# Talking-heads attention: the first twelve tiles mix the queries instead of the scores

## The chip, the cores and the metric

The kernel runs on one core of one Trainium2 chip. The metric is the device time of one execution in microseconds (us); smaller is better.

## The reference

Attention with mixed heads, then a feed-forward layer, for batch 8, 12 heads, 448 positions and head size 64; the layer goes from 768 to 2048 and back.

```python
scores = 1/sqrt(64) * q @ k.T                          # per batch and head: 448 x 448
scores = einsum('bhij,hg->bgij', scores, w_pre)        # 12 x 12: heads mixed before the softmax
attn   = exp(scores - max) / sum(exp(scores - max))
attn   = einsum('bhij,hg->bgij', attn, w_post)         # heads mixed after it
x      = (attn @ v) with heads side by side            # 3584 x 768
out    = relu(x @ w_in)**2 @ w_out
```

## The kernel before

**Loads.** q, k and v of a batch come in three parts of four heads each, on GpSimd's DMA queue, which turns f32 into bf16 (L76). TensorE transposes two pairs of heads at a time (`turn_unit`, L153), and ScalarE or VectorE copies the result to `qT` and `kT` (L155): 128 partitions are two heads of 64, and there are six such pairs.

**Scores.** A batch's 448 queries are cut into blocks of 128 (the fourth has 64). `score_burst` multiplies a block's queries of some head pairs with all keys (L280, L286 for the fourth block) and copies each head's 128 x 448 scores to a tile `S` (L290 on ScalarE, L292 on VectorE). There are two S buffers, so a block's copies wait until the block two before has been read.

**Tiles.** The mixing works on tiles of 10 queries; a batch has 45 (numbered on through the batches, tile 45 is the first of batch 1). `gather` (L309, L312; SyncE's DMA queue) copies the 10 x 12 rows of 448 scores of a tile from S, where a query is a partition, to a tile `G`, where each of 120 rows is one query of one head. There are twelve G buffers, and the program order has the gather of tile i + 10 behind step i. `mix` then needs one matmul with a 120 x 120 matrix `pre`, which holds `w_pre` for each of the ten queries (L320), an exp with row sums on ScalarE (L323), a reciprocal on VectorE (L325), and on GpSimd the product of that with the matrix `post` (L327). Four steps later (`LAG`), `unmix` multiplies exp with it by four matmuls (L340) and VectorE copies the result (L342). The tiles of the fourth block hold the heads in another order and have their own versions of `pre`, built from further small loads of w_pre (`col_pre`, L99; L107 to L119).

**The rest.** Every 15 tiles `av_unit` multiplies with v (L169). The feed-forward layer of a batch (`ffn1_unit`, L213, L219, L223; `ffn2_unit`, L247) fills TensorE between the tiles of a later batch, by a list with weights in time; batch 0's first half is put in early, from step 21 on (`EARLY`).

**Order.** TensorE's and GpSimd's instructions are issued in the order in which the program writes them; those of the other engines are ordered by a scheduler. A loop over steps emits, for step i: the loads due (`at_load`; GpSimd), `mix` of tile i, units due, filler, `unmix` of tile i - 4, the gather, and, at positions set by `FIRST` and `BURSTS`, half a score burst for the block after the one being gathered. Before the loop, batch 0's q and k are transposed, its first two blocks scored and copied, and ten gathers issued:

```python
        for x in range(2):
            score_burst(0, 1, [3 * x, 3 * x + 1, 3 * x + 2])
        for x in range(AHEAD):
            gather(steps[x])
```

The k and q loads of batch 1 go to the buffers of batch 0's, so they wait for its transposes; w_in (`w1`) and w_out (`w2`) are loaded in eight parts each, at the steps of `W1_AT` and `W2_AT`.

Of the kernel before, what the change touches and what calls it, by code (L numbers as in the profile page):

```python
# [8 lines left out]
BF16 = mybir.dt.bfloat16  # L9
F32 = mybir.dt.float32  # L10
# [33 lines left out]
def kernel(  # L44
# [33 lines left out]

    staged, vs = {}, {}
    staged[0] = (stage_tile("qst", 1), stage_tile("kst", 1))  # L80
    load(staged[0][1], k, 0, 0, 4)
    ident = consts.tile([P, P], BF16, name="ident")
    masks.make_identity(nc, ident[:, :])
    load(staged[0][0], q, 0, 0, 4)
    for x in (4, 8):
        load(staged[0][1], k, 0, x, x + 4)
        load(staged[0][0], q, 0, x, x + 4)

    def split(n0, n):

        rows = [(0, 0, [[0, n0], [H, H]], H * n0)] if n0 else []
        if n > n0:
            rows += [(H * n0 + HALF * (n - n0) * c, HALF * H * c, [[0, n - n0], [H, HALF]], HALF * (n - n0)) for c in range(2)]
        return rows

    def wcol(w, name, eng, n0, n):
        t = consts.tile([P, H], F32, name=name)
        for o, src, ap, rows in split(n0, n):
            eng.dma_start(out=t[o:o + rows, 0:H],  # L99
                          in_=bass.AP(tensor=w.tensor, offset=w[0, 0:1].offset + src, ap=ap + [[1, H]]))  # L100
        return t

    def stripes(name, n0, n):
        t = consts.tile([P, IQ], F32, name=name)
        rg = H * n
        if n0:
            nc.vector.tensor_reduce(out=t[0:rg, 0:n0], in_=ident[0:rg, 0:H * n0].rearrange("p (i h) -> p i h", h=H),  # L107
                                    axis=mybir.AxisListType.X, op=ALU.add)
        if n > n0:
            nc.vector.tensor_reduce(out=t[0:rg, n0:n], in_=ident[0:rg, H * n0:rg].rearrange(  # L110
                "p (c i h) -> p i c h", c=2, h=HALF), axis=mybir.AxisListType.XY, op=ALU.add)
        return t

    def pre_matrix(x, eng, n0, n):
        col = wcol(w_pre, f"col_pre{x}", eng, n0, n)
        st = stripes(f"istripe{x}", n0, n)
        rg = H * n
        t = consts.tile([P, IQ, H], BF16, name=f"pre{x}")
        nc.vector.tensor_tensor(out=t[0:rg, 0:n, :], in0=st[0:rg, 0:n].unsqueeze(2).to_broadcast([rg, n, H]),  # L119
                                in1=col[0:rg, :].unsqueeze(1).to_broadcast([rg, n, H]), op=ALU.mult)  # L120
        return t[:, :, :].rearrange("p i g -> p (i g)"), st

    pre, istripe = pre_matrix(0, nc.sync, IQ, IQ)
    col_post = wcol(w_post, "col_post", nc.scalar, IQ, IQ)
# [12 lines left out]
    w2 = [wts.tile([P, FT // 4, DMODEL], BF16, name=f"w2_{x}") for x in range(4)]  # L137

    qTs, kTs, xts, h2ts, ats = {}, {}, {}, {}, {}

    def turn_unit(b, which, u, eng=None):

# [126 lines left out]
    def score_burst(b, blk, pairs):  # L269

        if (b, blk) not in Sb:
            Sb[(b, blk)] = work.tile([P, H, S], BF16, name="S", tag="S", bufs=2)
        sb = Sb[(b, blk)]
        got = []
        for p in pairs:
            for hh in range(2):
                rs = slice(64 * hh, 64 * hh + 64)
                ps = bank("s_ps")
                if blk < 3:
                    nc.tensor.matmul(ps[:, 0:S], lhsT=qTs[b][rs, p, P * blk:P * blk + P], rhs=kTs[b][rs, p, :],  # L280
                                     start=True, stop=True)
                got.append((2 * p + hh, ps))
            for c in range(2 if blk == 3 else 0):
                for hh in range(2):
                    rs = slice(64 * hh, 64 * hh + 64)
                    nc.tensor.matmul(got[2 * p + hh][1][64 * c:64 * c + 64, 0:S], lhsT=qTs[b][rs, 3 * c + p, P * blk:S],  # L286
                                     rhs=kTs[b][rs, 3 * c + p, :], start=True, stop=True)
        for h, ps in got:
            if h % 2 == 0 or (b == 0 and h in (3, 9)):
                nc.scalar.copy(out=sb[:, h, :], in_=ps[:, 0:S])  # L290
            else:
                nc.vector.tensor_copy(out=sb[:, h, :], in_=ps[:, 0:S])  # L292

    def rows_of(t):
        return H * min(IQ, S - IQ * t)

    def gather(s):

        b, t = s
        g = work.tile([P, S], BF16, name="G", tag="G", bufs=AHEAD + 2)  # L300
        x, end = IQ * t, min(IQ * t + IQ, S)
        while x < end:
            blk = x // P
            n = min(end, P * blk + P) - x
            o, y = H * (x - IQ * t), x - P * blk
            sb = Sb[(b, blk)]
            dst = g[o:o + H * n, :]
            if blk < 3:
                nc.sync.dma_start(out=dst, in_=sb[y:y + n, :, :])  # L309
            else:  # L310
                for c in range(2):
                    nc.sync.dma_start(out=g[o + HALF * n * c:o + HALF * n * c + HALF * n, :],  # L312
                                      in_=sb[64 * c + y:64 * c + y + n, 0:HALF, :])
            x += n
        Gs[s] = g

    def mix(s):
        n = rows_of(s[1])
        ps = bank("m_ps")
# [39 lines left out]
        if not filler:  # L359
            owed[0] = min(owed[0], 0.0)  # L360

    blocks = [(b, blk) for b in range(B) for blk in range(4)]
    steps = [(b, t) for b in range(B) for t in range(NT)]
    with tc.manual_schedule(engines={PE, POOL}):
        for x in range(4):
            if x < 3:
                turn_unit(0, 1, x)
                turn_unit(0, 0, x, nc.scalar.copy)
            if x > 0:
                score_burst(0, 0, [2 * x - 2, 2 * x - 1])  # L370
        for x in range(2):
            score_burst(0, 1, [3 * x, 3 * x + 1, 3 * x + 2])
        for x in range(AHEAD):
            gather(steps[x])
        pres = {}
        for t in range(NT):
            n = min(IQ, S - IQ * t)
            key = (max(0, min(n, 3 * P - IQ * t)), n)
            if key not in pres.values():
                pres[t] = key  # L380
        pres = {t: pre if key == (IQ, IQ) else pre_matrix(t, nc.sync, *key)[0] for t, key in pres.items()}
        loads = {}

        def at_load(i, f, *args):
            loads.setdefault(i, []).append(lambda: f(*args))

        for x in range(3):
            load_v(0, x)
# [21 lines left out]
        for i in range(-1, len(steps) + LAG):  # L410
            for f in loads.get(i, []):
                f()
            if i < 0:
                continue
            s0 = steps[i] if i < len(steps) else None
            s1 = steps[i - LAG] if i >= LAG else None
            if s0:
# [15 lines left out]
            if s1:  # L433
# [4 lines left out]
                        at_step(i + 2, u)  # L438
                if t1 == NT - 1:
                    at_step(i + 2 if b1 else FFN2_AT, (0, lambda b1=b1: filler.extend(ffn_units(b1))))  # L440
            if i + AHEAD < len(steps):
                gather(steps[i + AHEAD])
                b2, t2 = steps[i + AHEAD]
                blk2 = max(x for x in range(4) if FIRST[x] <= t2)
                nxt = 4 * b2 + blk2 + 1
                first = BURSTS[blk2]
                if 1 < nxt < len(blocks) and t2 - FIRST[blk2] in first:
                    x = first.index(t2 - FIRST[blk2])
# [37 lines left out]
```

## Time and profile before

| | us |
|---|---|
| median of 3 runs | 623.85 (623.54 to 625.07) |
| profiled execution | 621.52 |
| its span in the profile | 619.6 |
| TensorE busy | 568.9 (92%) |
| VectorE busy | 403.5 (65%) |
| ScalarE busy | 380.9 (61%) |
| GpSimd busy | 333.0 (54%) |
| gathers (L309, L312) | 368 transfers of 105.0 or 52.5 KB and some smaller |

PE is TensorE's matmuls and PEld its weight loads, DVE is VectorE, ACT ScalarE, POOL GpSimd, SP SyncE. Busy times are unions of intervals, and engines run side by side. Rows of digits cut the span in 40 slices of 15.5 us and give tenths of it busy; PEclk is the clock granted to TensorE in tenths of full speed, DMA the mean busy share of 16 DMA engines (in a short stretch it can go over 1, as packets overlap). In the chain of waits each line has the start, the length and what the end of the kernel waited for; "idle ... <-" or "waited" names what came last. A group's line gives the form, the count, then the busy time in us, the mean of one in ns, and the idle time before it.

### The profile page before, as it was taken

To read this page: it belongs to the slowest core of one execution; us is meant where nothing else is said; L and a number is where in the kernel's file an instruction comes from. 1 tells how busy PE (TensorE), PEld (TensorE's weight loads), DVE (VectorE), ACT (ScalarE), POOL (GpSimd) and SP (SyncE) were. 2 spreads that over 40 slices of the span, in tenths; PEclk is the share of its full clock that TensorE was granted. 3 is DMA by queue.
4 is the path that set the end of the run, shared out by engine and by line. 5 is a ranking of instruction groups with operands and counts; after the bars stand their busy time and mean duration, and the time that the engine had idled before them with its cause. 6 is when DMAs were issued, how large, how long until landed. Compare 5 with 4: busy or idle time off the path is not lost.

```text
span 619.6 us, 17165 instructions
## 1 busy us (share of the span) xinstructions
PE 568.9 (92%) x5960; PEld 366.6 (59%) x5960; DVE 403.5 (65%) x998; ACT 380.9 (61%) x1107; POOL 333.0 (54%) x742
## 2 busy tenths in 40 slices
PE   3657697989999999999999999999999999998996
PEld 2225475656656666656666666656665666665553
DVE  2448574498877778777767778777767677665011
ACT  2746586666677656776577557776578557861410
POOL 4434589736277623794287623793286425751640
PEclk9769799899999999999999999999999999999999
DMA  9999789649856965488446965488543655422002
GB/s 123 144 187 193 146 167 211 96 100 164 190 105 105 143 142 119 76 144 164 106 95 108 150 135 110 80 142 161 119 87 63 118 129 104 87 51 73 7 26 77
DMA packets 91104, 73.51 MB, mean 119 GB/s; under 512 B 7048, under 2 KB 87432, under 8 KB 91016
## 3 DMA queue, kind: packets, MB, share of 16 engines
q1 hardware_dynamic: 52102, 49.59, 34.6%
q0 software_dynamic: 38784, 22.81, 28.7%
q8 instruction: 47, 0.77, 0.5%
q14 instruction: 41, 0.34, 0.1%
q10 hardware_dynamic: 130, 0.01, 0.0%
HBM read 45.64 MB, written 11.01 MB: 91 GB/s over the span
## 4 chain that ended last, share of the span: by engine, by line
PE 79%; DMA 10%; ACT 4%; DVE 2%; POOL 2%; issue 1%; SPq 1%; ACTq 0%; DVEq 0%; POOLq 0%
PE o_ps L247 24%; PE h_ps L213 21%; PE at_ps L340 11%; PE m_ps L320 10%; DMA G<-S 9%; PE ot_ps L169 6%; PE s_ps L280 3%; PE tr_ps L153 3%; ACT S L290 2%; ACT e L323 1%; DMA col_pre<-in_w_pre_dram 1%; PE s_ps L286 1%; DVE at L342 1%; POOL h L223 1%; SPq L99 1%
## 5 line engine op out<-in xcount | busy, mean ns | idle before, releaser
L342 DVE CAST at<-at_ps 112x480 bf16<-112x480 f32 x360 | 227.9, 649 | 69.3 <-PE at_ps L340 68.4
L327 POOL TENSOR_SCALAR pn<-post,rc 120x120 bf16<-120x120 bf16 x360 | 130.5, 365 | 219.4 <-DVE rc L325 130.3
L323 ACT ACTIVATE e<-m_ps 120x448 bf16<-120x448 f32 x360 | 195.6, 549 | 77.1 <-PE m_ps L320 77.1
L213 PE MATMUL h_ps<-xt,w 128*128 128x448 bf16 (+2 forms) x960 | 168.4, 316 | 0.9 <-ACT e L323 0.3
L340 PE MATMUL at_ps<-pn,e 120*128 120x120 bf16 (+1 forms) x1440 | 136.3, 218 | 13.3 <-ACT S L290 11.6
L320 PE MATMUL m_ps<-G,pre 120*120 120x448 bf16 x360 | 131.6, 367 | 12.2 <-DMA G<-S 8.3
L340 PEld LDWEIGHTS <-e 120*128 120x128 bf16 (+1 forms) x1440 | 106.0, 99 | 59.9 <-ACT S L290 15.0
L247 PE MATMUL o_ps<-w,h 128*128 128x384 bf16 x768 | 139.3, 327 | 0.0
L223 POOL TENSOR_TENSOR h<-hr 128x384 bf16<-128x384 f32 (+2 forms) x160 | 111.1, 696 | 29.7 <-ACT hr L219 26.3
L213 PEld LDWEIGHTS <-w 128*128 128x128 bf16 x960 | 84.4, 98 | 55.7 <-issue 5.0
L219 ACT ACTIVATE hr<-h_ps 128x448 f32<-128x448 f32 (+2 forms) x160 | 75.7, 475 | 57.0 <-PE h_ps L213 32.4
L290 ACT CAST S<-s_ps 128x448 bf16<-128x448 f32 x175 | 81.5, 552 | 34.5 <-PE s_ps L280 19.2
L247 PEld LDWEIGHTS <-h 128*128 128x128 bf16 x768 | 73.6, 98 | 48.2 <-issue 5.0
L292 DVE CAST S<-s_ps 128x448 bf16<-128x448 f32 x161 | 90.4, 615 | 16.3 <-DMA G<-S 13.2
L325 DVE RECIPROCAL rc<-sm 120x1 f32<-120x1 f32 x360 | 57.0, 159 | 57.0 <-ACT e L323 46.2
L323 ACT ACTIVATION_READ_ACCUMULATOR e<-m_ps 120x1 f32 x360 | 75.1, 209 | 0.0
L320 PEld LDWEIGHTS <-pre 120*120 120x120 bf16 x360 | 48.6, 135 | 33.1 <-DMA G<-S 14.2
L253 DVE COPY osb<-o_ps 128x384 f32<-128x384 f32 x56 | 31.2, 557 | 55.4 <-PE o_ps L247 55.1
L280 PE MATMUL s_ps<-kT,qT 64*128 64x448 bf16 x288 | 42.0, 364 | 5.1 <-ACT hr L219 3.2
L169 PE MATMUL ot_ps<-at,v 112*64 112x150 bf16 x1152 | 42.0, 228 | 4.4 <-DVE at L342 4.3
L175 ACT CAST xt<-ot_ps 128x450 bf16<-128x450 f32 (+1 forms) x48 | 25.5, 533 | 32.9 <-PE ot_ps L169 32.9
L169 PEld LDWEIGHTS <-v 112*64 112x64 bf16 x1152 | 38.4, 109 | 8.1 <-issue 6.7
(30 smaller groups left out, 248.5 us busy)
## 6 DMA issues: line engine op xcount, KB each, us to landing
G<-S SPq DMA_DIRECT2D x288, 105.0 KB
kst<-in_k_dram POOLq DMA_DIRECT2D x24, 224.0 KB, 5.6
qst<-in_q_dram POOLq DMA_DIRECT2D x24, 224.0 KB, 5.5
v<-in_v_dram POOLq DMA_DIRECT2D x24, 224.0 KB, 6.8
G<-S SPq DMA_DIRECT2D x80, 52.5 KB
w<-in_moe_w_in_dram POOLq DMA_DIRECT2D x8, 384.0 KB, 8.6
w<-in_moe_w_out_dram POOLq DMA_DIRECT2D x8, 384.0 KB, 8.0
out_dram<-osb SPq DMA_DIRECT2D x8, 336.0 KB
```

Source lines behind the costliest of these rows:

```text
L169: nc.tensor.matmul(ps[64 * hh:64 * hh + 64, TQ * y:TQ * y + TQ], lhsT=vs[b][0:PR, g, r, :], rhs=at[0:PR, r, g, :], start=(y == 0 and r == ...
L213: nc.tensor.matmul(ps[:, 0:n], lhsT=w1[ft // 4][:, c2, ft % 4 * 128:ft % 4 * 128 + 128], rhs=xts[b][:, c2, n0:n1], start=(c2 == 0), stop=( ...
L219: nc.scalar.activation(out=hr[:, 0:n], in_=ps[:, 0:n], func=ACT.Relu)
L223: nc.gpsimd.tensor_tensor(out=dst[:, x - o:y - o], in0=hr[:, x - n0:y - n0], in1=hr[:, x - n0:y - n0], op=ALU.mult)
L247: nc.tensor.matmul(ps[:, 0:384], lhsT=lhsT, rhs=w2[ft // 4][:, ft % 4, nt * 384:(nt + 1) * 384], start=(ft == 0), stop=(ft == FT - 1))
L290: nc.scalar.copy(out=sb[:, h, :], in_=ps[:, 0:S])
L292: nc.vector.tensor_copy(out=sb[:, h, :], in_=ps[:, 0:S])
L320: nc.tensor.matmul(ps[0:n, 0:S], lhsT=pres[max(x for x in pres if x <= s[1])][0:n, 0:n], rhs=Gs.pop(s)[0:n, :], start=True, stop=True)
L323: nc.scalar.activation(out=e[0:n, 0:S], in_=ps[0:n, 0:S], func=ACT.Exp, scale=SCALE, accum_out=sm[0:n, 0:1])
L327: nc.gpsimd.tensor_scalar(out=pn[0:n, :], in0=post[0:n, :], scalar1=rc[0:n, 0:1], scalar2=1.0, op0=ALU.mult, op1=ALU.mult)
L340: nc.tensor.matmul(ps[:, RG * r:RG * r + RG], lhsT=e[0:n, PR * r:PR * r + P], rhs=pn[0:n, :], start=True, stop=True)
L342: nc.vector.tensor_copy(out=ats[(b, third)][0:PR, :, :, IQ * tl:IQ * tl + IQ], in_=ps[0:PR, 0:R * RG].rearrange("p (r g i) -> p r g i", r= ...
```

## The change

Mixing the heads' scores with w_pre is the same as mixing the queries first: for output head g, the query of each head h is multiplied by w_pre[h, g], and one product over all heads and their 64 dimensions gives the mixed score. Tiles 0 to 11 (120 queries of batch 0) now do that. `mix_queries` writes `qmix`: per pair of heads and query, twelve versions of the query, one for each g, as a product of `qT` with `wrep`, which holds w_pre's row of each partition's head. Nine such instructions replace the scores of these tiles: for each of three `u` (two pairs of heads), queries 0 to 39 and 40 to 79 on VectorE and 80 to 119 on GpSimd. `mix` of these tiles is then six matmuls, one for each pair of heads, that add up in PSUM; they need no S copies and no gather. qmix lies in the buffers of w_out's first three quarters, which are loaded from step 26 on.

For batch 0 the remaining 328 queries make three blocks of 128, starting at queries 120, 240 and 320, where there were four; none of its tiles is split between blocks, and none has the other order of heads. Its first block is scored in three parts: before step 0, in step 0 and in step 1. Gathers start in the program order of step 6, two in each step until they are ten ahead.

At the start, q is loaded before k in each part, q's copies move to VectorE and k's to ScalarE, and v's loads stand ahead of the mixing on GpSimd. One `col_pre` load stays; the versions of `pre` for the other order of heads are made at step 22 by three small matmuls and copies. `wrep` is loaded by two transfers of 384 rows of 48 bytes each.

```diff
-FIRST = [0, 13, 26, 39, NT]
-BURSTS = [[5, 8], [5, 8], [6], [0, 3]]
+FUSED = 12
+FQ = FUSED * IQ
+QB = (0, 40, 80, FQ)
+STARTS = {0: (FQ, 2 * FQ, S - 128)}
+FIRST = {0: (FUSED, 2 * FUSED, 3 * FUSED)}
+BURSTS = {0: ([5, 8], [5, 8], [3, 6])}
+for _b in range(1, B):
+    STARTS[_b], FIRST[_b], BURSTS[_b] = (0, 128, 256, 384), (0, 13, 26, 39), ([5, 8], [5, 8], [6], [0, 3])
+GATHERS_AT = 6
...
+    wrep = consts.tile([P, NPAIR, H], F32, name="wrep")
+    for hh in range(2):
+        nc.sync.dma_start(out=wrep[64 * hh:64 * hh + 64, :, :],
+                          in_=bass.AP(tensor=w_pre.tensor, offset=w_pre[0, 0:1].offset + H * hh,
+                                      ap=[[0, 64], [2 * H, NPAIR], [1, H]]))
...
+    def mix_queries(u, part, eng):
+        a, n = QB[part], QB[part + 1] - QB[part]
+        eng.tensor_tensor(out=qmix[u][:, :, a:a + n, :],
+                          in0=qTs[0][:, 2 * u:2 * u + 2, a:a + n].unsqueeze(3).to_broadcast([P, 2, n, H]),
+                          in1=wrep[:, 2 * u:2 * u + 2, :].unsqueeze(2).to_broadcast([P, 2, n, H]), op=ALU.mult)
...
     def mix(s):
...
-        nc.tensor.matmul(ps[0:n, 0:S], lhsT=pres[max(x for x in pres if x <= s[1])][0:n, 0:n], rhs=Gs.pop(s)[0:n, :], start=True, stop=True)
+        if b == 0 and t < FUSED:
+            for p in range(NPAIR):
+                nc.tensor.matmul(ps[0:n, 0:S], rhs=kTs[b][:, p, :],
+                                 lhsT=qmix[p // 2][:, p % 2, IQ * t:IQ * t + IQ, :].rearrange("p i g -> p (i g)"),
+                                 start=(p == 0), stop=(p == NPAIR - 1))
+        else:
+            m = pres[max(x for x in pres if x <= t)] if b else pre
+            nc.tensor.matmul(ps[0:n, 0:S], lhsT=m[0:n, 0:n], rhs=Gs.pop(s)[0:n, :], start=True, stop=True)
...
-        for x in range(4):
-            if x < 3:
-                turn_unit(0, 1, x)
-                turn_unit(0, 0, x, nc.scalar.copy)
-            if x > 0:
-                score_burst(0, 0, [2 * x - 2, 2 * x - 1])
-        for x in range(2):
-            score_burst(0, 1, [3 * x, 3 * x + 1, 3 * x + 2])
-        for x in range(AHEAD):
-            gather(steps[x])
+        for x in range(3):
+            load_v(0, x)
+        for u in range(NPAIR // 2):
+            turn_unit(0, 0, u)
+            mix_queries(u, 0, nc.vector)
+            mix_queries(u, 1, nc.vector)
+            if u == 1:
+                score_burst(0, 0, [0, 1])
+            if u < 2:
+                mix_queries(u, 2, nc.gpsimd)
+            turn_unit(0, 1, u, nc.scalar.copy)
...
             if i < 0:
+                mix_queries(2, 2, nc.gpsimd)
                 continue
+            if i == NT // 2:
+                for (_, n), (t, order) in orders.items():
+                    half_pre(n, t, order)
...
-            if i + AHEAD < len(steps):
-                gather(steps[i + AHEAD])
...
+            if i < 2:
+                score_burst(0, 0, [2 + 2 * i, 3 + 2 * i])
+            for _ in range(2 if i >= GATHERS_AT else 0):
+                if ahead[0] > min(i + AHEAD, len(steps) - 1):
+                    break
+                b2, t2 = steps[ahead[0]]
+                gather((b2, t2))
+                ahead[0] += 1
```

More of the change, by code (lines that the diff above doesn't have):

```diff
@@ L96, in wcol @@
-    def wcol(w, name, eng, n0, n):
+    def wcol(w, name, eng):
         t = consts.tile([P, H], F32, name=name)
-        for o, src, ap, rows in split(n0, n):
-            eng.dma_start(out=t[o:o + rows, 0:H],
-                          in_=bass.AP(tensor=w.tensor, offset=w[0, 0:1].offset + src, ap=ap + [[1, H]]))
-        return t
-    def stripes(name, n0, n):
-        t = consts.tile([P, IQ], F32, name=name)
-        rg = H * n
[L106 to L123, printed above, removed]
@@ L124 @@
-    col_post = wcol(w_post, "col_post", nc.scalar, IQ, IQ)
+        src = bass.AP(tensor=w.tensor, offset=w[0, 0:1].offset, ap=[[0, IQ], [H, H], [1, H]])
+        eng.dma_start(out=t[0:RG, 0:H], in_=src)
+        return t
+    col_pre = wcol(w_pre, "col_pre", nc.sync)
+    istripe = consts.tile([P, IQ], F32, name="istripe")
+    nc.vector.tensor_reduce(out=istripe[0:RG, :], in_=ident[0:RG, 0:RG].rearrange("p (i h) -> p i h", h=H),
+                            axis=mybir.AxisListType.X, op=ALU.add)
@@ new lines, with half_order @@
+    pre = consts.tile([P, IQ, H], BF16, name="pre")
+    nc.vector.tensor_tensor(out=pre[0:RG, :, :], in0=istripe[0:RG, :].unsqueeze(2).to_broadcast([RG, IQ, H]),
+                            in1=col_pre[0:RG, :].unsqueeze(1).to_broadcast([RG, IQ, H]), op=ALU.mult)
+    pre = pre[:, :, :].rearrange("p i g -> p (i g)")
+    def half_order(x, n0, n):
+        t = consts.tile([P, RG], BF16, name=f"order{x}")
+        o, rg = H * n0, H * n
+        if n0:
+            nc.vector.tensor_copy(out=t[0:rg, 0:o], in_=ident[0:rg, 0:o])
+        nc.vector.tensor_copy(out=t[0:rg, o:rg].rearrange("p (c i h) -> p c i h", c=2, h=HALF),
+                              in_=ident[0:rg, o:rg].rearrange("p (i c h) -> p c i h", c=2, h=HALF))
+        return t
@@ new lines, with half_pre @@
+    orders, pres = {}, {0: pre}
+    for t in range(3 * P // IQ, NT):
+        n0, n = max(0, 3 * P - IQ * t), min(IQ, S - IQ * t)
+        if (n0, n) not in orders:
+            orders[(n0, n)] = (t, half_order(t, n0, n))
+    def half_pre(n, t, order):
+        rg = H * n
+        ps = bank("pre_ps")
+        nc.tensor.matmul(ps[0:rg, 0:rg], lhsT=order[0:rg, 0:rg], rhs=pre[0:rg, 0:rg], start=True, stop=True)
+        pres[t] = consts.tile([P, RG], BF16, name=f"pre{t}")
+        nc.vector.tensor_copy(out=pres[t][0:rg, 0:rg], in_=ps[0:rg, 0:rg])
```

50 lines of the change are left out of this document (21 added, 29 removed).

## The prediction

> **What bounds the kernel now.** I read the page first, then busy time by stages, the chain of waits of the first 75 us, the waits by engine, and single rows for prices. The page:
>
> ```profile
> span 619.6 us, 17165 instructions
> ...
> PE   3657697989999999999999999999999999998996
> ...
> PEclk9769799899999999999999999999999999999999
> DMA  9999789649856965488446965488543655422002
> ```
>
> PE is full from about the tenth slice (15.5 us each) to the end; before that it has holes, and there the DMA row shows 9. The stages, cut at tiles 0, 12, 23, 31 and 55 (the starts of their L320 matmuls in the timeline: 25.44, 43.85, 57.06, 72.27 and 112.31):
>
> ```profile
> core 0: us, PE busy (x) PEld busy (x) DVE busy (x) ACT busy (x) POOL busy (x), PEclk, DMA share, GB/s
> 0.00:25.40 25.40, 10.12 (x120) 5.73 (x120) 8.63 (x27) 10.98 (x20) 9.85 (x19) 0.96 1.02 134
> 25.40:43.90 18.50, 10.52 (x57) 5.13 (x58) 7.62 (x23) 9.10 (x30) 8.53 (x18) 0.59 0.97 173
> 43.90:57.00 13.10, 11.02 (x213) 7.98 (x211) 10.93 (x30) 8.71 (x27) 6.64 (x15) 1.00 1.00 192
> 57.00:72.30 15.30, 8.33 (x93) 6.18 (x90) 8.23 (x20) 8.36 (x28) 6.79 (x16) 0.86 0.89 178
> 72.30:112.30 40.00, 35.41 (x488) 28.93 (x487) 24.25 (x62) 29.55 (x102) 34.24 (x83) 0.97 0.96 169
> 112.30:600.00 487.70, 479.07 (x4915) 304.12 (x4913) 340.46 (x832) 314.18 (x902) 266.99 (x594) 1.00 0.58 109
> ```
>
> From 112.3 on PE is busy 98% of the time: whatever the start gains or loses is carried to the end. In the first four rows (72.3 us) PE is idle 32.3 us and DMA is at 0.89 to 1.02. The chain says on what, and the waits say through whom:
>
> ```profile
> 17.18 2.21 ACT S L290 x6
> 19.38 6.01 DMA G<-S
> ...
> 32.31 7.65 DMA G<-S
> ...
> 40.65 11.28 DMA G<-S
> ...
> 64.65 5.75 DMA G<-S
> ```
>
> ```profile
> ACT S L290 <- DMA G<-S: 15.2, 3, 7.9
> ```
>
> The gathers hurt twice. Tile 0 can start only when all S copies of block 0 and a first gather (6.01) are through. And S has two buffers: the S copies of a new block wait, in ACT's and DVE's order, until the gathers out of the block two before have landed; exp and unmix copies queue behind them. That is 15.2 us on ACT in three waits (32 to 40, near 57, 65 to 70.5).
>
> **The change part by part.** Five rows give the prices; the second number after the bar is the mean in ns:
>
> ```profile
> L119 DVE TENSOR_TENSOR pre<-istripe,col_pre 120x120 bf16<-120x120 f32 x3 | 0.8, 283 | 7.8 <-DMA col_pre<-in_w_pre_dram 7.8
> ...
> L119 DVE TENSOR_TENSOR pre<-istripe,col_pre 96x96 bf16<-96x96 f32 x1 | 0.3, 255 | 0.3 <-DVE istripe L110 0.3
> ```
>
> ```profile
> L223 POOL TENSOR_TENSOR h<-hr 128x384 bf16<-128x384 f32 x112 | 92.4, 825 | 22.4 <-ACT hr L219 19.1
> ...
> L223 POOL TENSOR_TENSOR tails<-hr 128x64 bf16<-128x64 f32 x128 | 37.0, 289 | 0.0
> ```
>
> ```profile
> 201.82 1.30 PE L213 MATMUL h_ps<-xt,w 128*128 128x448 bf16 x6
> ```
>
> *Mixing the queries.* Nine tensor_tensors of 960 elements, six on DVE, three on POOL. DVE's slope is (283-255)/24 = 1.17 ns an element, so 283 + 840 x 1.17 = 1.26 us each; POOL's is (825-289)/320 = 1.68, so 289 + 896 x 1.68 = 1.79 us each.
>
> *Their weights, wrep.* Two SP transfers, 768 rows of 48 B, take the place of seven col_pre transfers (336 such rows). The first DVE mix waits for both. No row shows this transfer. Lower bound: the first col_pre (120 rows, issued 0.75) was used at 4.67, 3.9 us later; the second wrep would be issued at about 2.6 and with three times the rows land at about 8. Upper bound: from 8.0 to 13.5 us, with the q/k/v loads filling the engines, that queue moved 292 packets, 252 of them such rows, 46 a us; 768 rows from 4.5 us on then land at 21. I take 13 us: the nearest row is the col_pre issued at 4.88, which landed at 12.68, 7.8 us under the same loads. The Trainium skill ("DMA: Bandwidth & Descriptors", section "Why a DMA increments its semaphore by 16 and not by 1") says that a transfer runs on as many engines, up to 16, as divide both sides' slowest dimension: 16 for wrep's 64 partitions against 10 or fewer for col_pre's rows. By that the per-row pace is too pessimistic; no run here shows it yet.
>
> *First tile.* After wrep, DVE does two mixes, a qT copy (0.61), two mixes, a copy, one mix, before PE can end tile 0: 5 x 1.26 + 2 x 0.61 = 7.5 us. Nothing is queued behind it that is due sooner; kT copies now run on ACT. On POOL the b=1 k and q loads stand behind two of its mixes: they are issued near 19 us instead of 15.8, and are first needed at step 14 (tile 14, near 44 us). Whether DVE and POOL mixes run side by side no row shows: between 0 (side by side) and 2 x 1.79 = 3.6 us (POOL first each time) I put one POOL mix, 1.8 us, on the path. The Trainium skill ("SBUF — State Buffer", section "SBUF: two separate sides") speaks against the change here: a DVE instruction with two SBUF inputs and a GpSimd instruction that reads SBUF lock each other out of one port pair for the whole instruction; by it the term is 3.6 and not 1.8. So: 13 + 7.5 + 1.8 + 0.7 for the last cold matmuls = 23.0 for tile 0, against 25.44.
>
> *Tiles 0 to 11.* Six matmuls each. Warm price: the six of L213 at 201.82 have the same 448 columns, and PE's next instruction starts at 202.96, so 0.19 us a matmul, 1.14 a tile; an unmix (202.96 to 203.17) adds 0.21. The granted clock was 0.59 in the second stage above, with PE half idle; here PE is dense, so I count tile 1 and the eight score matmuls beside it at half clock (6 x 0.38, and twice the 0.93 of the four at 13.67: 4.2 us), and ten tiles at full clock: 11.4 + 8 unmixes 1.7 + 12 score matmuls 1.5 (six at 74.71 took 0.74) = 14.6. Tile 12 starts at 23.0 + 4.2 + 14.6 = 41.8, against 43.85: 2 us ahead. The 60 extra matmuls (11.4 us) take the place of PE's idle time; without that cover the change loses them.
>
> *Tiles 12 to 28.* Their gathers can be issued as soon as the first block is copied, near 28.5 us (at 0.86 us each, by the gathers' issue rows), 13 us before they are used. The three waits for a gather at tiles 17, 18 and 20 (0.69 + 0.70 + 0.65) go; a little work comes in (two more S copies on DVE, three small matmuls and copies for half_pre). Before, 18.96 us; I take 18.3, DVE being busy 10.9 of 13.1 us there already. Tile 29 at 60.1 against 62.81.
>
> *The wait at tile 29 to 31.* Before, block (1,0) goes into the buffer of tiles 26 to 38, whose last gather is issued at 64.65 and lands at 70.41; tile 29 to tile 31 takes 9.46 us, with ACT idle 5.34. After, batch 0 has three blocks, the buffer is that of tiles 24 to 35, three gathers earlier, and none of batch 0's gathers is split in two. The gather of tile 35 needs the G buffer of tile 23 (there are twelve), is issued at about 55 and lands, with the same 6 to 8 us, at 61 to 63. I leave 1 us of wait: 4.5 instead of 9.46. Sum at tile 31: 2.7 + 5.0 = 7.7 us ahead.
>
> *A second way to that sum.* The stage is full of DMA: twelve gathers of 105 KB fewer are 1.26 MB, at 171 GB/s (the mean of the first 72 us from 3 us on) 7.4 us.
>
> *Behind tile 31* PE's instructions stand in the same order as before. DMA is at 0.96 and POOL busy 34.24 of 40 us up to tile 55, so loads that now crowd closer may give 1.2 us back. Net 6.5 us: the profiled execution goes from 621.52 to 615.0, and the median of the runs, 2.3 us above that execution, from 623.85 to 617.3.
>
> **The rivals.** *Slower: wrep lands late.* At 21 us tile 0 is through at 32, tile 12 at 50.8 (7 us late), the b=1 loads and all W1 loads are issued 8 us later, since POOL takes them in order behind its mixes, and the wait at tile 31 only gives back 5. That is about 3 us slower, 626.8; it decides from wrep at 18 us on. For it: 46 rows a us beside the loads. Against: those transfers were still being issued until 8.01.
>
> *No change.* Lead given back up to tile 55, because the 17 weight, k, q and v loads of that stage set its time: about 623.5. For: DMA 0.96. Against: PE and POOL hold 35.41 and 34.24 of the 40 us by themselves.
>
> *More.* wrep by 9 us and mixes side by side: tile 0 at 17.2, tile 12 at 36, gathers started near 23 and the wait at tile 31 gone: 11 to 12 us faster, 612.
>
> *Little.* The gather wait at tile 29 stays at 5 us since the gathers start 9 us later than now: 3 us faster, 621.
>
> **How the numbers follow.** Forecast 4 to 9 us faster 0.55, more 0.13, little 0.10, no change 0.10, slower 0.12. 0.3% is 1.9 us, about what a measurement of this kernel can tell from no change: faster 0.78, same 0.10, slower 0.12. The range 612.0 to 624.5 leaves out the slower case and the far end of "more".
>
> **What would show it.** wrep's end as the DVE mix's start (13); first fused matmul's tile done near 23; tile 12 near 42; no ACT wait over 2 us on a gather before 75 us; tile 31 near 64.6; from there the same distance to the end. The forecast is wrong if the first DVE mix starts after 18, if the fused matmuls cost 0.38 us throughout, or if tile 55 has lost the lead of tile 31.

## The result, and the profile after

The changed kernel took 617.16 us (median of 4 runs, 614.54 to 619.12) against 623.69 (4 runs, 621.81 to 625.07): a ratio of 0.9895, interval 0.9848 to 0.9941. Four further sets of runs, each with its own runs of before, stand behind the experiments; in one of them the changed kernel was measured again. The profiled execution took 617.85 us (before: 621.52).

The page after, same rows as before:

```profile
span 616.1 us, 17210 instructions
...
PE   3797988898999999999999999999999999998996
...
PEclk9797998999999999999999999999999999999999
DMA  8997999559647955587547955597544755422002
```

PE's holes are fewer, but not gone: the 7 in the fourth slice (46 to 62 us) is where the lead is spent. The stages, cut at the first fused matmul (16.2) and at tiles 12, 23, 31 and 55 by the start of their matmuls:

```profile
core 0: us, PE busy (x) PEld busy (x) DVE busy (x) ACT busy (x) POOL busy (x), PEclk, DMA share, GB/s
0.00:16.20 16.20, 5.87 (x100) 4.32 (x100) 7.46 (x18) 4.72 (x7) 10.67 (x17) 1.00 0.84 104
16.20:40.80 24.60, 20.85 (x131) 12.17 (x126) 17.27 (x31) 12.90 (x36) 16.19 (x24) 0.86 1.07 158
40.80:59.50 18.70, 14.27 (x218) 10.23 (x216) 12.57 (x35) 10.44 (x33) 6.63 (x16) 0.82 0.84 166
59.50:67.70 8.20, 7.38 (x88) 5.62 (x88) 7.01 (x19) 7.41 (x26) 5.90 (x15) 1.00 0.82 137
67.70:108.30 40.60, 35.97 (x489) 29.72 (x487) 24.68 (x64) 29.60 (x104) 35.52 (x87) 0.96 1.05 189
```

Tiles 12 to 22 (third row) take 18.7 us where they took 13.1, with PE busy 14.27 and its clock down to 0.82; tiles 23 to 30 (fourth row) take 8.2 instead of 15.3. The chain of waits says why (start, length, what was waited for):

```profile
2.56 8.24 DMA wrep<-in_w_pre_dram
10.92 3.84 DVE w L163 x2
14.76 0.55 DVE qT L181
15.33 3.84 DVE w L163 x2
...
42.93 7.99 DMA G<-S
50.95 0.54 ACT S L317
51.53 0.53 PE s_ps L307
52.06 0.56 PE m_ps L355
52.61 3.14 PE ot_ps L195 x47
```

The waits from 15 to 73 us, by engine, have one entry for S on ACT, and PE's next score matmul waits behind it:

```profile
ACT S L317 <- DMA G<-S: 4.3, 1, 4.3
...
PE s_ps L307 <- ACT S L317: 3.7, 1, 3.7
```

Before it was 15.2 us in three waits; now it is one, of 4.3 us, at a place where the prediction had none: ahead of tile 20. The S copies of batch 0's last block go into the buffer that tiles 12 to 23 are gathered from. The last of those gathers, tile 23's, was issued at 38.36, and the copies could start at 50.95, 12.6 us later. The chain names a later gather there (issued at 42.93); the semaphore on which ACT waits last is that of tile 23's gather. Its updates are in the trace: behind a first one at 39.55, nine came from 46.20 to 48.52 and the last at 50.85, which ended the wait. After the stall PE comes back at half clock: the 47 matmuls of `ot_ps` take 3.14 us, and the granted clock is 0.50 from 52.6 to 55.7.

Start of the first matmul of four tiles, in us, in every profile of this study (the kernels are explained below). The medians are from different sets of runs, so they are compared by their ratios; w1_late's ratio leaves out one slow run, of 621.75 us.

| kernel | tile 12 | tile 20 | tile 31 | tile 55 | median | ratio to before |
|---|---|---|---|---|---|---|
| before | 43.85 | 51.97 | 72.27 | 112.31 | 623.69 | 1 |
| after | 40.77 | 51.99 | 67.71 | 108.33 | 617.16 | 0.9895 (0.9848 to 0.9941) |
| after, again | 39.84 | 51.02 | 66.40 | 105.73 | 615.18 | 0.9896 (0.9856 to 0.9935) |
| own_before | 40.37 | 51.64 | 67.08 | 111.84 | 618.65 | 0.9954 (0.9933 to 0.9975) |
| own_after | 40.21 | 47.35 | 61.24 | 102.70 | 613.15 | 0.986 (0.9831 to 0.9889) |
| w1_late | 40.01 | 47.60 | 63.23 | 103.27 | 616.27 | 0.9909 (0.9873 to 0.9946) |
| mix_first | 37.85 | 49.58 | 64.98 | 104.33 | 615.72 | 0.99 (0.9869 to 0.9931) |
| wrep_one | 39.97 | 50.26 | 65.95 | 106.55 | 616.17 | 0.9921 (0.9892 to 0.9949) |
| wrep_pe | 38.04 | 49.07 | 64.83 | 105.43 | 615.81 | 0.9886 (0.9851 to 0.992) |
| dup_thin | 41.01 | 56.98 | 72.16 | 111.64 | 623.31 | 0.9996 (0.9975 to 1.0017) |
| dup12 | 40.66 | 64.32 | 80.50 | 121.52 | 631.51 | 1.015 (1.012 to 1.0179) |
| own_mix | 36.07 | 43.89 | 57.47 | 101.11 | 609.9 | 0.9805 (0.9776 to 0.9834) |
| best | 33.76 | 40.96 | 54.77 | 99.80 | 608.1 | 0.9766 (0.9735 to 0.9796) |
| best_w1 | 33.46 | 41.28 | 54.79 | 100.26 | 610.89 | 0.9819 (0.9788 to 0.9849) |

Two profiles of the same kernel (after, after again) differ by 0.9 us at tile 12 and 2.6 at tile 55, so smaller differences between rows say nothing. Behind tile 55 all kernels have the same program order, yet the 14 profiles take 507.2 to 510.8 us from there to the end. Most of that lies between tiles 55 and 90, where the clock granted to TensorE differs even between two executions of one kernel, here after and after again:

```profile
108.33:153.40 45.07, 39.83 (x484) 26.12 (x482) 36.92 (x95) 30.51 (x95) 22.71 (x57) 1.00 0.75 127
```

```profile
105.73:153.50 47.77, 43.21 (x484) 27.35 (x482) 36.86 (x95) 30.76 (x96) 23.65 (x60) 0.93 0.73 122
```

So "whatever the start gains or loses is carried to the end" holds only within about 3 us for a single execution. Why the clock is lower in one of them is open.

### The profile page after: what moved, and what is told of

It is laid out like the page before. It is cut to its first block, busy times and chain, and to the rows that moved or that the text cites. A ratio compares the mean times of both kernels' runs of the same rounds, so it can differ in the third digit from the quotient of the medians.

```text
span 616.1 us, 17210 instructions
## 1 busy us (share of the span) xinstructions
PE 577.5 (94%) x6011; PEld 375.7 (61%) x6011; DVE 412.7 (67%) x1002; ACT 378.5 (61%) x1103; POOL 340.9 (55%) x745
## 4 chain that ended last, share of the span: by engine, by line
PE 81%; DMA 8%; DVE 4%; ACT 3%; POOL 1%; issue 1%; SPq 0%; ACTq 0%; DVEq 0%
PE o_ps L273 23%; PE h_ps L239 21%; PE at_ps L375 11%; PE m_ps L355 10%; DMA G<-S 7%; PE ot_ps L195 7%; PE s_ps L307 3%; PE tr_ps L179 3%; PE m_ps L350 2%; ACT e L358 2%; DVE w L163 1%; DMA wrep<-in_w_pre_dram 1%; PE s_ps L313 1%; DVE at L377 1%; ACT S L317 1%
## 5 line engine op out<-in xcount | busy, mean ns | idle before, releaser
L375 PE MATMUL at_ps<-pn,e 120*128 120x120 bf16 (+1 forms) x1440 | 134.9, 216 | 0.5 <-ACT hr L245 0.2
L355 PE MATMUL m_ps<-G,pre 120*120 120x448 bf16 x348 | 125.2, 360 | 4.7 <-ACT S L317 2.7
L317 ACT CAST S<-s_ps 128x448 bf16<-128x448 f32 x171 | 79.9, 547 | 27.1 <-PE s_ps L307 20.2
L355 PEld LDWEIGHTS <-pre 120*120 120x120 bf16 x348 | 46.3, 133 | 25.8 <-issue 13.2
L195 PE MATMUL ot_ps<-at,v 112*64 112x150 bf16 x1152 | 44.9, 237 | 4.4 <-DVE at L377 4.3
L195 PEld LDWEIGHTS <-v 112*64 112x64 bf16 x1152 | 41.2, 115 | 8.3 <-issue 6.7
```

The costliest lines, as they stand in the source:

```text
L195: nc.tensor.matmul(ps[64 * hh:64 * hh + 64, TQ * y:TQ * y + TQ], lhsT=vs[b][0:PR, g, r, :], rhs=at[0:PR, r, g, :], start=(y == 0 and r == ...
L355: nc.tensor.matmul(ps[0:n, 0:S], lhsT=m[0:n, 0:n], rhs=Gs.pop(s)[0:n, :], start=True, stop=True)
L375: nc.tensor.matmul(ps[:, RG * r:RG * r + RG], lhsT=e[0:n, PR * r:PR * r + P], rhs=pn[0:n, :], start=True, stop=True)
```

## The experiments

The question: the lead of 3.1 us at tile 12 is gone at tile 20, yet at tile 31 it is 4.6. What ate it, and what gave it back?

**The S buffer.** In both kernels the scores of batch 0's third block get a buffer of their own, so that no copy of this block waits for a gather; nothing else is changed. It lies in the third and fourth quarter of `w2`, which is loaded later.

```diff
...
-            Sb[(b, blk)] = work.tile([P, H, S], BF16, name="S", tag="S", bufs=2)
+            if (b, blk) == (0, 2):
+                Sb[(b, blk)] = w2all[:, 8:16, :].rearrange("p c m -> p (c m)")[:, 0:H * S].rearrange(
+                    "p (h s) -> p h s", h=H)
+            else:
+                Sb[(b, blk)] = work.tile([P, H, S], BF16, name="S", tag="S", bufs=2)
```

> The changed kernel with a buffer of its own for the scores of batch 0's third block (in w_out's buffers, loaded later), so that its S copies at steps 19 and 22 wait for no gather, nor those of block (1,0) at step 29. Theory A (the changed kernel lost its lead at tiles 19 to 23 since the S copies stand in ACT's and DVE's order until the gather of tile 23 has landed): the 4.3 us of ACT idle at 46.6 to 50.9 is gone, tile 23 starts near 54 and not 59.45, the v matmuls behind it run at full clock (1.7 us, not 3.1), the end is 3 to 5 us earlier than the changed kernel, a ratio to the kernel before of 0.982 to 0.985. Theory B (the DMA engines set the time of this stage and the S buffer is only where it shows): tiles 22 to 30 wait for their own gathers instead, tile 31 stays within 1 us of 67.7, ratio 0.988 to 0.991.

> The kernel before with the same buffer of its own for the scores of batch 0's third block, nothing else changed. Theory A (the S buffer's wait costs the time): ACT's waits of 7.9 us at 32 to 40 and 5.3 us at 65 to 70.5 are gone and the end is 7 to 10 us earlier, as much as the change gains. Theory B (the DMA engines set it): tiles 10 to 20 wait for their own gathers, tile 20 still starts near 50 and tile 31 near 70; the end is 0 to 3 us earlier.

Changed kernel: 0.986, between the two theories' ranges and nearer the first's; the wait is gone, tile 20 comes 4.6 us earlier and tile 31 6.5. No stall, no half clock; the same `ot_ps` matmuls in the chain of own_after:

```profile
48.01 1.76 PE ot_ps L196 x48
```

So the wait for the gather of tile 23 is what held tiles 20 to 31. In the kernel before, the same edit brought 0.9954 only. Its S waits up to 73 us went as well, and PE waits more for its own tiles' gathers (17.1 us, where before has 11.6):

```profile
PEld L325 <- DMA G<-S: 17.1, 15, 5.8
...
PE m_ps L325 <- DMA G<-S: 12.1, 8, 5.1
```

Even so it starts tile 31 at 67.08, 5.2 us ahead of before and as early as the changed kernel. From tile 29 to tile 31 it takes 3.70 us, the changed kernel 3.60, before 9.46: this answers the second half of the question, since it is the S wait of block (1,0) that the changed kernel's three blocks remove there. But the chain of own_before has the next S wait soon behind:

```profile
77.25 5.57 DMA G<-S
...
82.92 0.54 ACT S L295
```

From tile 41 to tile 42 it takes 4.3 us instead of 0.8, and at tile 55 0.5 us of its lead is left. So there the edit moved the wait to a later tile. In the changed kernel's profile with the own buffer no such wait follows.

**The loads beside that gather.** The last four of eight w_in loads move from steps 11, 15, 19 and 23 to steps 20 to 23; the first of them no longer run beside the gathers of tiles 12 to 23.

```diff
-W1_AT = (1, 3, 5, 7, 11, 15, 19, 23)
+W1_AT = (1, 3, 5, 7, 20, 21, 22, 23)
```

> The changed kernel with the second half of w_in's loads (384 KB each) moved from steps 11, 15, 19, 23 to steps 20 to 23. Theory (beside these loads a gather gets half the DMA engines' packets, and so the gather of tile 23 lands 12.5 us after its issue): it lands near 46 to 47 and not at 50.9, the S copies at step 19 wait under 1 us, tile 23 starts near 55 and not 59.45; the loads then press on the gathers of tiles 30 to 38, so the end is 1 to 4 us earlier. Rival (the gather's landing is set by its own queue): it lands at 50 as before, nothing earlier than 1 us, or later since the loads for step 32 come late.

The gather of tile 23 lands 9.7 us after its issue (at 46.49) instead of 12.5, the wait ahead of tile 20 is gone, and tile 20 starts at 47.60: the loads are a good part of what made the gather late. From tile 29 to 31 it takes 5.71 us instead of 3.60, so some is given back where the loads are bunched now; at tile 55 the profile is still 5.1 us ahead of after. The median did not follow (0.9909; its interval and that of after again, run beside it, cover each other). The profiled execution is the fastest of its eight (612.3 us), so why the others do not show the lead is open. By the trace the mechanism holds; as a cure it is not shown to be worth anything.

**Mixing order, and the two engines.** The queries of tiles 0 to 3 are mixed first for all pairs, and all nine mixes stand on VectorE.

```diff
-            mix_queries(u, 1, nc.vector)
...
-            if u < 2:
-                mix_queries(u, 2, nc.gpsimd)
...
-                mix_queries(2, 2, nc.gpsimd)
+                for part in (1, 2):
+                    for u in range(NPAIR // 2):
+                        mix_queries(u, part, nc.vector)
```

> The changed kernel with the query mixes in another order: the three mixes for queries 0 to 39 first, the six others behind them, all nine on DVE and none on POOL. Theory of the shared lock (a DVE mix and a POOL mix shut each other out: 1.16 us and 2.76 us in pairs): every DVE mix takes 1.16 us, the third one ends near 17.5 and tile 0's last matmul starts there, not at 20.95; tile 12 near 37.5; at the end 1 to 3 us faster than the changed kernel, since the gather wait at tile 20 moves with the gathers. Rival (the broadcast operands make a DVE mix slow by itself): mixes of 1.9 to 2.8 us, tile 0 no earlier, the end the same or later.

The timeline of after, the first mixes on each engine (start, length; x2 is two instructions in one line):

```profile
10.92 3.84 DVE L163 TENSOR_TENSOR w<-qT,wrep 128x960 bf16<-128x960 bf16 x2 [3.14 <-DMA wrep<-in_w_pre_dram]
...
10.97 2.78 POOL L163 TENSOR_TENSOR w<-qT,wrep 128x960 bf16<-128x960 bf16 x1 [2.71 <-DMA wrep<-in_w_pre_dram]
```

Taken singly: DVE 10.92 to 12.08, POOL 10.97 to 13.75, DVE 12.00 to 14.76. POOL's ends 1.67 us after DVE's first, and DVE's second 1.01 us after POOL's: they take turns. With POOL out of it, mix_first's timeline has five in a row, 1.08 us from one to the next, and each of the nine takes 1.15 to 1.16:

```profile
16.49 5.42 DVE L163 TENSOR_TENSOR w<-qT,wrep 128x960 bf16<-128x960 bf16 x5
```

Tile 12 came 2.9 us earlier; in the median nothing can be measured (0.99). The wait ahead of tile 20 is still there, 4.7 us instead of 4.3, but by the table it does not eat the lead: the gathers were issued earlier too, and 2.4 us are left at tile 20, 2.7 at tile 31 and 4.0 at tile 55 (2.0, 1.4, 1.4 and 1.4 against after again). From tile 55 on this profile takes 510.5 us against 507.7, at a clock of 0.93 up to tile 90. So whether the edit is worth 1 or 2 us is not shown either way.

**wrep's transfer.** In wrep_one it is one load of 128 rows of 576 bytes and two copies on VectorE, in place of 768 rows of 48 bytes. In wrep_pe there is none: twelve matmuls of a selecting matrix with `col_pre` make it in PSUM (with w_pre rounded to bf16).

```diff
+    wall = consts.tile([P, NPAIR, 2, H], F32, name="wall")
+    nc.sync.dma_start(out=wall[:, :, :, :].rearrange("p n c g -> p (n c g)"),
+                      in_=bass.AP(tensor=w_pre.tensor, offset=w_pre[0, 0:1].offset, ap=[[0, P], [1, H * H]]))
     wrep = consts.tile([P, NPAIR, H], F32, name="wrep")
     for hh in range(2):
-        nc.sync.dma_start(out=wrep[64 * hh:64 * hh + 64, :, :],
-                          in_=bass.AP(tensor=w_pre.tensor, offset=w_pre[0, 0:1].offset + H * hh,
-                                      ap=[[0, 64], [2 * H, NPAIR], [1, H]]))
+        nc.vector.tensor_copy(out=wrep[64 * hh:64 * hh + 64, :, :], in_=wall[64 * hh:64 * hh + 64, :, hh, :])
```

> The changed kernel with wrep made from one load of all of w_pre to every partition (128 rows of 576 bytes instead of 768 of 48) and two small DVE copies. Theory (the many short rows hold up the q and k loads beside them as well as the first mix): the row load lands by 6 us, the first k part by 8 and not 10.34, the first mix starts at 7.9 to 8.5 and not 10.92, tile 0 ends 2 to 3 us earlier, the end 1 to 3 us earlier. Rival (the k load is late for another reason): k lands at 10.3 as before and only the mix on the first q part moves; tile 0 at most 1 us earlier.

```diff
...
+        for h in range(H):
+            o = 64 * (h % 2)
+            nc.tensor.matmul(ps[o:o + 64, H * (h // 2):H * (h // 2) + H], lhsT=sel[0:H, h, :], rhs=wsm[0:H, :],
+                             start=True, stop=True)
+        nc.vector.tensor_copy(out=wrep[:, :, :].rearrange("p n g -> p (n g)"), in_=ps[:, 0:NPAIR * H])
...
```

> The changed kernel with wrep made on the chip: twelve small matmuls pick w_pre's rows out of the col_pre that is loaded anyway, one DVE copy; the weights are rounded to bf16 on the way. No wrep transfer is left. Theory (a transfer that spreads one small piece of DRAM over all partitions holds up the loads beside it, whatever its rows): the second load (first k part) lands near 8 us and not at 10.1 to 10.3, the last v near 18.3 and not 19.1; the first mix starts at 7.9 to 8.2 instead of 10.92, tile 0 ends 2.5 to 3 us earlier, tile 12 at 38; the end 1 to 3 us earlier. Rival (the order q before k, or the loads themselves, set the k landing): k still lands at 10; the mixes still start 3 us earlier, but tile 0 moves by 1 us at most.

The changed kernel was run once more beside wrep_pe, w1_late and best:

> The changed kernel itself, beside the other three of this job. Its ratio to the kernel before was 0.9895 (0.985 to 0.994). The theory that its own profiled execution (3.7 us faster at its end, 5.5 us ahead at tile 33) is a typical one gives 0.990 to 0.994; the theory that the medians' 6.5 us are typical gives 0.988 to 0.990.

It came out at 0.9896 (0.9856 to 0.9935): the second theory's, though the interval covers both.

Fewer, longer rows were no better, which neither theory of wrep_one had: wall landed near 8.9, but q's first part only at 9.1 (6.1 in after), k's at 10.1, and the first mix still started at 10.96. Without the transfer k's first part landed at 7.57 instead of 10.34, and the first mix started at 8.27. The stretch from 4 to 10 us, first in after, then in wrep_pe (last column GB/s, the one before it DMA share):

```profile
4.00:10.00 6.00, 0.96 (x16) 0.74 (x16) 1.49 (x7) 0.00 (x0) 4.26 (x7) 1.00 0.69 79
```

```profile
4.00:10.00 6.00, 2.48 (x48) 2.04 (x50) 4.15 (x13) 0.91 (x1) 5.98 (x8) 1.00 1.27 160
```

While wrep moves, the q and k loads beside it get half of their pace. As with mix_first, the earlier start (tile 12 at 38.04) was not seen in the median, 0.9886 against 0.9896, though the profile keeps 2.9 us of lead over after up to tile 55.

**Twelve gathers put back.** In dup12 a copy of each gather of tiles 12 to 23 into a place that nobody reads stands right ahead of it in SP's queue (not behind it, as the texts on record have it); in dup_thin a copy of 12 of its 120 rows.

```diff
...
+            if b == 0 and t < 2 * FUSED:
+                nc.sync.dma_start(out=again[o:o + H * n, S * (t % 6):S * (t % 6) + S], in_=sb[y:y + n, :, :])
             if blk < 3:
                 nc.sync.dma_start(out=dst, in_=sb[y:y + n, :, :])
```

> The changed kernel, with the gathers of tiles 12 to 23 issued twice: each is followed by one more transfer of the same 120 rows of S into the buffer of the last quarter of w_out, which nobody reads before w_out is loaded there. So the 12 x 105 KB (1.26 MB) of DMA that the change took out are put back, with nothing else of the change undone. Theory A (the prediction's second way: the stage is full of DMA, and the change gains by the bytes that it takes out; 1.26 MB at 171 GB/s is 7.4 us): the last gather of the first block lands 4 to 8 us later, the S copies of the last block of batch 0 wait 8 us or more on ACT instead of 4.3, tile 31 starts 4 us or more later than in the changed kernel (66.4 to 67.7 there), and the time is 620 to 622, ratio 0.995 or more. Theory B (the gain is in the start and in the distance of the S buffer, the transfers lie in time that the tiles do not need): the wait grows by less than 2 us, tile 31 starts at 66 to 69, ratio 0.988 to 0.992.

> The changed kernel with twelve more transfers, one behind each gather of tiles 12 to 23, as in the kernel that issued these gathers twice (631.5 us, ratio 1.015; tile 31 at 80.5 us against 67.7), but each copies 12 rows of S instead of 120: the same number of issues on SP's queue, a tenth of the bytes (0.13 MB). It tells which of the two that kernel paid for. Theory A (the queue: a gather is issued in 0.77 to 2 us, one behind the other, and the last gather of the first block is issued 12 x 0.85 = 10 us later whatever it moves): that gather issued at 48 or later instead of 38.4, tile 31 at 74 to 79, ratio 1.002 to 1.012. Theory B (the bytes: 1.26 MB in a stage full of DMA): the last gather of the first block is issued at 47 or later all the same, but lands 6 to 7 us after its issue instead of 12.5 since the loads beside it have ended by then, tile 31 at 68 to 72, ratio 0.990 to 0.998.

The twelve short transfers alone take the whole gain back (0.9996, between what the two theories gave); with all their bytes the kernel is slower than before (1.015, 631.5 us, where the first theory had 620 to 622). The chain of dup_thin, and then that of dup12 (SPq is SP issuing a gather):

```profile
35.68 7.79 DMA G<-S
43.48 0.80 SPq L339
...
48.69 1.15 SPq L339
...
53.08 2.77 DMA G<-S
55.94 0.54 ACT S L318
```

```profile
55.80 0.80 SPq L339
56.60 6.45 issue
...
63.28 0.54 ACT S L318
```

SP issues one transfer behind the other, 0.73 us at best and up to 2 us. It also waits: the program gives SP's transfers eight semaphores in turn, so an issue waits until the transfer eight places earlier has landed. In dup_thin's chain the issue at 43.48 waits for the transfer issued at 35.68. The gather of tile 23 is issued at 38.36 in after, 48.69 in dup_thin, 55.80 in dup12, and lands 12.5, 6.9 and 7.2 us later; the S copies start at 50.95, 55.94 and 63.28, and tile 31 at 67.71, 72.16 and 80.50: 4.5 and 12.8 us behind after, for S copies 5.0 and 12.3 behind. Tile 31 follows the S copies almost one for one. A gather thus has two prices in this stage, its place in SP's queue and its bytes: twelve places cost (0.9996 - 0.9895) x 623.7 = 6.3 us, the rest of the bytes (1.015 - 0.9996) x 623.7 = 9.6; by the intervals of the ratios the first can be off by 3 us and the second by 2. This is the price of more gathers in the changed kernel; the kernel before issued its first twelve from 19.38 on, before the first could be issued here (27.11), so it is not the gain read backwards.

**The edits together.** own_mix has the own buffer and the mixing order; best has wrep made by TensorE besides, and best_w1 the late w_in loads on top. Their edits are those shown above.

> The changed kernel with two edits: the scores of the last block of batch 0 go into a buffer of their own (the place of w_out's third and fourth quarter), and the queries of tiles 0 to 3 are mixed first, with all nine mixes on DVE. Alone, the first edit gave a ratio of 0.986 to before, the second moved tile 12 from 40.8 to 37.9 us, and its lead was lost in the wait for the gather of tile 23 before tile 31. Theory A (leads that are won ahead of tile 12 are lost only because of that wait; without it they reach the end): tile 12 near 37.5, tile 31 near 58.5, ratio 0.979 to 0.983. Theory B (the loads and gathers of the first 100 us set the time, whatever tile 12 does): tile 31 near 61 as with the first edit alone, ratio 0.985 to 0.988. The kernel with these two edits and wrep made by TensorE had 0.9766.

> Three edits together: own buffer for the third block's scores, mixes for queries 0 to 39 first and all on DVE, wrep made on the chip (weights rounded to bf16). If the gains add (5.6 us at the end for the own buffer by its profile, 3 us at tile 12 for the order of the mixes, up to 3 for wrep): tile 0 ends near 16, tile 12 near 35, tile 31 near 56, ratio to the kernel before 0.974 to 0.979. If the DMA engines bound the stage up to tile 31 once the S wait is gone, tile 31 stays at 59 to 61 with waits of PE on gathers, ratio 0.983 to 0.987.

> The best version so far (own buffer for the last block's scores, the queries of tiles 0 to 3 mixed first and all on DVE, wrep made by twelve small matmuls; 608.1 us, ratio 0.9766), with the last four of the eight w_in loads moved from steps 11, 15, 19 and 23 to steps 20 to 23. Theory A (the gathers of tiles 12 to 23 still land late because w_in is loaded beside them): tiles 20 to 31 come 1 to 2 us earlier, ratio 0.973 to 0.976. Theory B (with the own buffer nothing waits for these gathers any more, and the bunched loads hold up the gathers of tiles 26 to 35 or the first half's feed-forward instead): 0.976 to 0.982, tile 31 at 54 to 57.

Together the edits come through: own_mix 0.9805, best 0.9766, the fastest kernel of the study at 608.1 us, 2.3% under before. Two of the three showed nothing measurable alone. That they need the buffer to count is not shown: at tile 31 the three leads over after, 6.5, 2.7 and 2.9 us, simply add up to 12.1, and best has 12.9. The medians alone would add up to about 0.985, but their intervals are too wide to tell that from 0.9766. The late loads do not help any more (0.9819): tiles 12 to 31 come no earlier, and a gather in the chain of best_w1 now takes

```profile
52.71 14.40 DMA G<-w2all
```

beside the bunched loads; tile 45 starts 3.8 us later than in best (79.64 against 75.82).

A lead of 12.9 us at tile 31 (best against after) is 8.5 at tile 55. The own buffer has a price there: it lies where w_out goes, so GpSimd, which issues that load in program order, waits for the last gather out of the buffer. The waits of best from 15 to 73 us have

```profile
POOL w2all L239 <- DMA G<-S: 3.7, 1, 3.7
```

and the same wait is 0.9 us in own_after, 4.6 in own_mix and 6.6 in best_w1. From tile 42 to tile 45, where it falls, the leads over before shrink by 3.4 us (best), 0.5, 5.3 and 5.0. That is about as much, but no run has the buffer in another place.

## Why the prediction was right, and where it was not

The forecast of 617.3 stands beside 617.16, faster as forecast; but one term failed, and others made up for part of it. By its steps, in the profile:

*wrep, the mixes, tile 0: 23.0 forecast, 21.95 measured.* wrep landed near 10.8, not 13; the lower bound 8 and the nearest row's 13 straddle it, and the upper bound of 21, by the pace of a row, was far off. A mix takes 1.16 us on DVE (forecast 1.26). From the first mix to the end of the fifth, 10.92 to 20.91, are 5 x 1.16 + 2 x 0.55 = 6.9 us of DVE's own and 3.1 more: two POOL mixes on the path, not one (1.8). The Trainium skill's "SBUF — State Buffer", section "SBUF: two separate sides", which was weighed there, would have given 3.6, with the two engines locking each other out for a whole instruction; the trace agrees with it: 2.76 to 2.78 us in pairs against 1.16 alone. The term was 1.3 us too short, and the transfer's was 2.2 us too long.

*Tiles 0 to 11: 18.8 forecast (23.0 to 41.8), 18.8 measured (21.95 to 40.77).* Six warm fused matmuls took 1.14 us, as priced from the rows of `h_ps`; the six of tile 1, cold, 2.43.

*Tiles 12 to 28: 18.3 forecast, 23.34 measured (40.77 to 64.11).* This is the step that failed. "The three waits for a gather ... go" held for those waits, and "issued ... 13 us before they are used" held for PE. But the copies of block 2 also need the buffer that the gathers read, and that is free only when the last of twelve has landed, issued one behind the other on SP from 27.11 to 38.36. With "6 to 8 us" that is 44 to 46, ahead of the copies; the trace had 50.95. The term that was mis-sized is the gather's time to landing: 12.5 us here, 11.5 to 13.0 in the eight profiles that leave the loads and the number of gathers as they are. The chain shown in the prediction held the warning: its third gather is 11.28 us long, beside loads, as this one. That "no ACT wait over 2 us" would be left was wrong by the same step (4.3).

*Tiles 29 to 31: 4.5 forecast instead of 9.46, 3.6 measured.* This step held: block (1,0) finds its buffer free. own_before gets the same (3.7) with no mixed queries at all.

*Tile 31: 64.6 forecast, 67.71 measured;* 4.6 us ahead of before instead of 7.7. *Up to tile 55* 0.6 us were given back (40.62 against 40.04), not 1.2, and from there the distance to the end is 507.7 us against 507.3. The second profile of this kernel was 5.9 us ahead at tile 31 and 6.6 at tile 55, so the steps' sizes hold to 1 or 2 us.

So the profiled execution was forecast at 615.0 and took 617.85: 3.7 us faster than before's, not 6.5. The medians differ by 6.5; the ratio's interval allows 3.7 to 9.5. That the number was met to 0.1 us is chance; that the sign and the size were met rests on tile 0, the fused matmuls and the wait at tile 29, which were each about right.

*The second way* (1.26 MB at 171 GB/s, 7.4 us) had the right neighbourhood from too simple a reason: dup12 and dup_thin show that the queue's places count beside the bytes, and own_before reaches tile 31 as early with all gathers in place. No run has the mixed queries without the three blocks, or the blocks without them, so what each part of the change is worth alone is not shown.

*The rivals.* "Slower" fell with wrep at 10.8 (it needed 18). "No change", the lead given back up to tile 55, is not seen in after (0.6 us), but it is in own_before, which loses 4.7 of its 5.2 us there; best loses 4.4. "Little" had the right kind of event, a gather's wait that stays, at the wrong tiles: 20 instead of 29. "More" needed mixes side by side, which this pair of engines did not do; best gets beyond its 612 with POOL's mixes moved to DVE, the own buffer and an earlier wrep.

## What to carry to other kernels

When a transfer frees a buffer, forecast the buffer by the last transfer of its group: its place in the issuing queue plus the longest latency seen beside such loads, not the first one's issue and a mean. When a buffer wait is taken away, look for the next one: in own_before it came back at tile 42, and in best it became a wait of the load that needs the lent place. Follow a lead from tile to tile to the end: one of 2 or 3 us can be there up to tile 55 and still vanish in the median, when executions differ by as much through the granted clock; such an edit is not shown to be worthless. Elementwise work split over VectorE and GpSimd has to be priced as one engine's until a trace shows it side by side.

## What the runs showed of the hardware

- DVE's and POOL's `tensor_tensor` with both inputs in SBUF take turns by whole instructions: 1.16 us alone, 2.76 (DVE) and 2.78 (POOL) while the other runs.
- A small table read from DRAM into all partitions halves the pace of the loads beside it while it moves (79 against 160 GB/s from 4 to 10 us), with 768 rows of 48 bytes; 128 rows of 576 bytes held the loads up as well (q's first part 9.1 instead of 6.1 us). Why is open; the shortness of the 48-byte rows is not the reason.
- A gather of 120 rows of 896 bytes, the last of twelve, landed 12.5 us after its issue beside 384 KB loads, and 9.7 us after it when four of these loads came later (w1_late); it took 6.9 and 7.2 in dup_thin and dup12, which issue it 10 and 17 us later. Its parts do not land together: in after the last update of its semaphore is 2.3 us behind the one before.
- The clock granted to TensorE over the same 45 us of work was 1.00 in one execution of a kernel and 0.93 in another, which took 2.7 us longer for it; after a stall of about 4 us it was 0.50 for over 3 us.
- SP's issue of a gather takes 0.77 to 0.80 us at best, and that of dup_thin's transfers with a tenth of the rows 0.73: short ones are hardly cheaper in SP's queue.
